# Clustered attention and softplus feed-forward: the value product with its halves side by side

## The chip, the cores and the metric

The kernel runs on one core of a Trainium2 chip. Five engines with queues of their own work side by side: TensorE (PE) multiplies, VectorE (DVE), ScalarE (ACT) and GpSimd (POOL) do the rest, and SyncE (SP) issues the DMAs. The metric is the device time of one execution in microseconds; lower is better. Both kernels compute the same function from the same inputs.

## The reference

Queries and keys are given to the nearest of 16 centroids per head, a query attends only to keys of its own cluster, and the attention's output goes through a feed-forward layer with softplus:

```python
q_assign = np.argmax(np.einsum('bhsd,hcd->bhsc', q_n, c_n), axis=-1)
k_assign = np.argmax(np.einsum('bhsd,hcd->bhsc', k_n, c_n), axis=-1)
mask = q_assign[:, :, :, None] == k_assign[:, :, None, :]
scores = scale * np.matmul(q, k.transpose(0, 1, 3, 2))
scores = np.where(mask, scores, -1000000000.0)
scores = scores - np.max(scores, axis=-1, keepdims=True)
attn = np.exp(scores)
attn = attn / (np.sum(attn, axis=-1, keepdims=True) + 1e-09)
out = np.matmul(attn, v)
...
h = x @ w_in
g = np.maximum(h, 0.0) + np.log1p(np.exp(-np.abs(h)))
return g @ w_out
```

There are 4 batches of 8 heads, 768 tokens, 64 values a head; the layer goes from 512 to 2048 and back to 512. The weights arrive in 64 bits.

## The kernel before

**Halves.** To keep fp32 accuracy at the speed of fp16, a number is held as two fp16 numbers, a high and a low half. A product of two such numbers is three products: high by high, high by low, low by high, summed in PSUM.

**Tiles.** A tile is 128 queries of one head against all 768 keys; there are 192, taken in eight passes of 24 (half a batch's queries, all heads; three tiles a head). `scores` multiplies them on TensorE (line 1021, four products of 384 columns into two PSUM banks), VectorE takes the negative maximum (`negm`, line 1037), ScalarE the exponential (line 1048). The result p is split into halves `phl` by a cast (line 539, any of three engines) and a subtraction (line 529, VectorE or GpSimd), and for two tiles at a time a transposing DMA turns it into `pt`. The first 24 tiles stay in fp32 and are turned on TensorE (line 1065); their exponential also adds up the row's sum.

**Values.** `attend` multiplies pt by the values. For each of the six key blocks of a later tile there are three products (lines 1157 to 1159), all into the same 64 columns: p's high half by v's high half with a column of ones beside it (65 columns; the ones give the row's sum), p's high half by v's low half (64), p's low half by v's high half and ones (65). Six tiles, the three tiles of two heads, stand side by side in one PSUM bank, `mbank`; when the sixth is done VectorE forms 1 / (sum + 1e-9) (lines 1183 and 1185) and scales all six out of PSUM into `x32` (line 1192). The bank is taken for the next six after that.

**Similarities.** `nearest` compares a query or key block with the centroids. From batch 1 on, ten of the twelve blocks of a group take their high and low part in one product of 32 columns (line 761), which VectorE then adds (line 771); for the last two there is no room in the bank, and they take two products each (lines 763, 764).

**Feed-forward.** `ffn1` (lines 1236 to 1238) and `ffn2` (lines 1319 to 1321) run behind attention by about a pass, with softplus on ScalarE, VectorE and GpSimd; `store` adds up two halves (line 1339) and issues the output.

**Order.** Every operation is a step of a generator. A table of numbers, `SEQUENCE`, says which generator issues its next operation (and, by thousands, on which of its possible engines), so the order on every engine's queue is fixed in the program. `Order` follows the issue with a clock of its own; from that it puts warming products into TensorE's expected gaps (line 494, "fills"). Engines run their queues in order and wait on semaphores that the framework sets from the tiles that are read and written.

The start of the kernel prepares keys, queries and weights (rebuilding the 64-bit weights from integer pieces) while the first tiles run.

## Time and profile before

| | |
|---|---|
| Time, median of 3 runs | 825.71 us (824.12 to 825.8) |
| Profiled execution: span, first to last instruction | 824.5 us |
| TensorE busy | 809.5 us, 98% |
| VectorE busy | 647.6 us, 79% |
| ScalarE busy | 567.8 us, 69% |
| GpSimd busy | 444.5 us, 54% |

For the profiled execution the page gives the span alone; the whole time of the timed runs lies about 1.2 us above it. A busy TensorE is one with a product in flight; products overlap, so the step from one start to the next says what a product costs, not its duration. A share of the span is a mean over stages that differ; the rows below are read by stretch.

### The profile page before, as it was taken

What the parts mean: (1) busy time and instruction counts of PE and PEld (TensorE: products, weight loads), DVE (VectorE), ACT (ScalarE), POOL (GpSimd) and SP (SyncE); (2) the same over time, 40 slices, a digit from 0 to 9 for tenths busy, and PEclk for the clock granted to TensorE, in tenths of its full rate; (3) what the DMA queues carried; (4) which work ended last, traced back from release to release, by engine and by line L of the source; (5) the groups of instructions that cost most, each with busy time, mean ns of one, the idle gap of its engine ahead of it and who ended that gap; (6) DMA issues with size and microseconds to landing.
All of it is one profiled execution on the core that took longest, in us unless ns stands there. A gap on an engine that the chain in (4) does not pass through costs nothing.

```text
span 824.5 us, 19467 instructions
## 1 busy us (share of the span) xinstructions
PE 809.5 (98%) x7893; PEld 518.3 (63%) x7893; DVE 647.6 (79%) x1127; ACT 567.8 (69%) x987; POOL 444.5 (54%) x358
## 2 busy tenths in 40 slices
PE   8999988999999999999999999999999999999998
PEld 7888865655656565656565656656666565555553
DVE  8999999998898977898778888887587887743222
ACT  7999998998857667667565746785686664433530
POOL 4325444655367376777685465856777653522320
PEclk9999999999999999999999999999999999999999
DMA  9436999999979999999978989999969874640001
GB/s 327 161 85 168 214 201 228 205 225 177 207 153 187 180 195 205 195 211 193 180 141 155 173 174 183 211 212 175 201 135 169 163 135 103 123 84 14 26 2 38
DMA packets 386314, 134.27 MB, mean 163 GB/s; under 512 B 362672, under 2 KB 379056, under 8 KB 386224
## 3 DMA queue, kind: packets, MB, share of 16 engines
q1 hardware_dynamic: 386224, 133.03, 80.1%
q8 instruction: 61, 1.00, 0.5%
q14 instruction: 29, 0.24, 0.1%
HBM read 35.68 MB, written 6.29 MB: 51 GB/s over the span
## 4 chain that ended last, share of the span: by engine, by line
PE 79%; DMA 4%; DVE 3%; ACT 3%; POOL 1%; issue 1%; DVEq 0%; ACTq 0%; POOLq 0%
PE s L1021 11%; PE h L1236 9%; PE h L1237 9%; PE h L1238 9%; PE o L1321 9%; PE o L1319 9%; PE o L1320 9%; DMA pt<-phl 4%; PE mbank L1157 3%; PE mbank L1159 3%; PE mbank L1158 3%; DVE negm L1037 1%; ACT p L1048 1%; DVE phl L529 1%; ACT phl L539 1%
## 5 line engine op out<-in xcount | busy, mean ns | idle before, releaser
L1048 ACT ACTIVATE p<-s,negm 128x768 f32<-128x768 f32 x190 | 171.9, 908 | 77.9 <-DVE negm L1037 65.6
L1037 DVE TENSOR_REDUCE negm<-s 128x1 f32<-128x768 f32 x192 | 181.7, 951 | 35.4 <-PE s L1021 34.2
L529 POOL TENSOR_TENSOR phl<-p,phl 128x768 f16<-128x768 f32 x81 | 138.2, 1710 | 71.7 <-DVE phl L539 36.0
L1238 PE MATMUL h<-xT,wi 128*128 128x384 f16 x512 | 166.8, 326 | 0.0
L1237 PE MATMUL h<-xT,wi 128*128 128x384 f16 x512 | 166.8, 326 | 0.0
L1236 PE MATMUL h<-xT,wi 128*128 128x384 f16 x512 | 166.7, 326 | 0.0
L1021 PE MATMUL s<-kt,qt 128*128 128x384 f16 x768 | 156.1, 326 | 2.5 <-DVE phl L1111 1.4
L1321 PE MATMUL o<-wo,gh 128*128 128x512 f16 x384 | 146.0, 380 | 0.0
L1320 PE MATMUL o<-wo,gh 128*128 128x512 f16 x384 | 146.0, 380 | 0.0
L1319 PE MATMUL o<-wo,gh 128*128 128x512 f16 x384 | 146.0, 380 | 0.0
L1285 POOL TENSOR_TENSOR fg<-fg,fa 128x384 f32<-128x384 f32 x64 | 69.8, 1094 | 82.9 <-ACT fa L1281 74.9
L1157 PE MATMUL mbank<-vb,pt 128*128 128x65 f16 x1008 | 109.0, 193 | 3.0 <-DMA pt<-phl 3.0
L1158 PE MATMUL mbank<-vb,pt 128*128 128x64 f16 x1008 | 109.1, 192 | 0.0
L1159 PE MATMUL mbank<-vb,pt 128*128 128x65 f16 x1008 | 108.8, 194 | 0.0
L1157 PEld LDWEIGHTS <-pt 128*128 128x128 f16 x1008 | 93.7, 98 | 16.8 <-DMA pt<-phl 5.1
L1021 PEld LDWEIGHTS <-qt 128*128 128x128 f16 x768 | 71.9, 98 | 48.9 <-issue 3.5
L1158 PEld LDWEIGHTS <-pt 128*128 128x128 f16 x1008 | 93.1, 97 | 11.4
L1267 ACT ACTIVATE fa<-h 128x384 f32<-128x384 f32 x82 | 40.2, 491 | 80.7 <-PE h L1238 63.8
L529 DVE TENSOR_TENSOR phl<-p,phl 128x768 f16<-128x768 f32 x81 | 90.6, 1125 | 4.3 <-ACT phl L539 2.2
L1159 PEld LDWEIGHTS <-pt 128*128 128x128 f16 x1008 | 93.2, 97 | 0.0
L539 ACT CAST phl<-p 128x768 f16<-128x768 f32 x92 | 75.2, 828 | 8.3 <-DMA pt<-phl 7.7
L1280 ACT ACTIVATE fa<-fa 128x384 f32<-128x384 f32 x128 | 65.8, 522 | 11.2 <-DVE fa L1263 11.1
(176 smaller groups left out, 1474.0 us busy)
## 6 DMA issues: line engine op xcount, KB each, us to landing
wo<-in_moe_w_in_dram SPq DMA_DIRECT2D x16, 512.0 KB, 6.8
wo<-in_moe_w_out_dram SPq DMA_DIRECT2D x14, 512.0 KB, 4.5
rawk<-in_k_dram SPq DMA_DIRECT2D x16, 384.0 KB, 4.2
rawq<-in_q_dram SPq DMA_DIRECT2D x16, 384.0 KB, 4.4
rawv<-in_v_dram SPq DMA_DIRECT2D x16, 384.0 KB, 4.6
out_dram<-ot SPq DMA_DIRECT2D x24, 256.0 KB, 2.6
pt<-phl SPq DMA_TRANSPOSE x82, 5.9
wraw<-in_moe_w_out_dram SPq DMA_DIRECT2D x2, 512.0 KB, 4.6
```

Of the source, the lines that this page charges most:

```text
L529: [lambda e=e: e.tensor_tensor(dst, a, b, ALU.subtract) for e in (nc.gpsimd, nc.vector)],
L1021: nc.tensor.matmul(st[:, j, :SH], qt[:, s, i], kt[:, s, NT // 2 * j : NT // 2 * (j + 1)], start=(s == 0), stop=(s == 1),)
L1037: yield op("DVE", 950, lambda: nc.vector.tensor_reduce(negm, st[:, :, :SH], AX.XY, ALU.max, negate=True))
L1157: nc.tensor.matmul(av, pt[:, 0, c], vb[:, c, D : 2 * D + 1], start=(c == 0), stop=False)
L1158: nc.tensor.matmul(av[:, :D], pt[:, 0, c], vb[:, c, :D], start=False, stop=False)
L1159: nc.tensor.matmul(av, pt[:, 1, c], vb[:, c, D : 2 * D + 1], start=False, stop=(c == NT - 1))
L1236: nc.tensor.matmul(hp, w[0], x[0], start=(c == 0), stop=False)
L1237: nc.tensor.matmul(hp, w[0], x[1], start=False, stop=False)
L1238: nc.tensor.matmul(hp, w[1], x[0], start=False, stop=(c == NP - 1))
L1319: nc.tensor.matmul(po, g[0], wo[:, f, 0, 0], start=(f == f0), stop=False)
L1320: nc.tensor.matmul(po, g[0], wo[:, f, 0, 1], start=False, stop=False)
L1321: nc.tensor.matmul(po, g[1], wo[:, f, 0, 0], start=False, stop=(f == f0 + NF // 2 - 1))
```

## The change

The value product of the later 168 tiles takes two products a key block instead of three: p's high half by v's low and high halves side by side (128 columns), and p's low half by v's high half (64 columns, added onto the second half of the 128). The two 64-column parts that result are added by VectorE, for two tiles at a time, on the way out of PSUM (`TENSOR_REDUCE`, line 1255 of the new kernel). The bank is cut into two slots of two tiles that take turns. The column of ones goes; ScalarE adds up the row sums of every tile with the exponential. The scaling of a later group then works from SBUF to SBUF, on VectorE or GpSimd. In the later similarities all twelve blocks are joint: the joint results begin at column 8 of the bank, and VectorE adds them in two instructions, the first eight and then the last four, since the later sums overwrite what the first instruction has read. More operations may run on GpSimd (weight preparation, query scaling, masks). The last output tile is multiplied and stored in two parts, 384 and 128 columns. `SEQUENCE` is a new table throughout; the other rank tables are the same.

```diff
--- before.py
+++ after.py
+PAIR = 425
...
 SEQUENCE = [
-    0, 0, 0, 0, 0, 0, 0, 0, 0, 0, 1, 2, 4, 0, 1, 0, 6, 468, 469, 1001, 0, 468, 0, 0, 3, 1, 468, 2004, 1, 0, 468, 1,
...
+    665, 466, 466, 466, 466, 466, 665, 666, 666, 466, 466, 466, 667, 667,
 ]
...
-        vb = cpool.tile([P, 2, NT, 2 * D + 2], F16, name=f"vb{i}")
-        nc.vector.memset(vb[:, :, :, 2 * D :], 1.0)
-        VB.append(vb)
+        VB.append(cpool.tile([P, 2, NT, 2 * D], F16, name=f"vb{i}"))
...
+    def either(dve, pool, f, shared=True):
+
+        if not shared:
+            return op("DVE", dve, lambda: f(nc.vector))
+        return op(
+            ("DVE", "POOL"), (dve, pool), (lambda: f(nc.vector), lambda: f(nc.gpsimd)), shared=True, bias=BIAS
         )
...
-        if joint:
+        for lo, hi in ((0, 8), (8, joint)) if joint else ():
             yield op(
                 "DVE",
-                145 + 35 * joint,
-                lambda: nc.vector.tensor_reduce(sim[:, :joint], wide.rearrange("p c s l -> p c l s"), AX.X, ALU.add),
+                145 + 35 * (hi - lo),
+                lambda: nc.vector.tensor_reduce(
+                    sim[:, lo:hi], wide[:, lo:hi].rearrange("p c s l -> p c l s"), AX.X, ALU.add
+                ),
             )
...
             hk, ps = yield from bank("x", False, [P, 32, NCL], F32, f"sim_q{sfx}")
-            wide = ps[:, nx:].rearrange("p (c s) l -> p c s l", s=2)
+            wide = ps[:, 8:].rearrange("p (c s) l -> p c s l", s=2)
...
             od.drop(hk)
         yield op(
-            "POOL",
-            180 + 1290 * part,
-            lambda: nc.gpsimd.tensor_tensor(n2[:, :, :D], n1[:, :, :D], aq.to_broadcast([P, nx, D]), ALU.mult),
+            ("POOL", "DVE"),
+            (180 + 1290 * part, 130 + DQA * part),
+            [
+                lambda e=e: e.tensor_tensor(n2[:, :, :D], n1[:, :, :D], aq.to_broadcast([P, nx, D]), ALU.mult)
+                for e in (nc.gpsimd, nc.vector)
+            ],
             shared=True,
...
-        tot = {}
-        if whole(t):
-            if n // 2 not in sums:
-                sums[n // 2] = p2.tile([P, 2 * nt, 1], F32, tag="sum", name=f"sum_{n}", bufs=NP)
-            tot["accum_out"] = sums[n // 2][:, n % 2 * nt + i]
-        yield op("ACT", 1000 if whole(t) else 898, lambda: nc.scalar.activation(ex, st[:, :, :SH], AF.Exp, bias=negm, **tot))
+        if (n // 2, pi) not in sums:
+            sums[n // 2, pi] = p2.tile([P, 2 * nt, 1], F32, tag="sum", name=f"sum_{n}_{pi}", bufs=NP)
+        total = sums[n // 2, pi][:, n % 2 * nt + i]
+        yield op("ACT", 1000, lambda: nc.scalar.activation(ex, st[:, :, :SH], AF.Exp, bias=negm, accum_out=total))
...
-        if h % 2 == 0 and i == 0:
-            avs["k"] = yield from ring("m", 1)
-            avs["t"] = mbank[:, : 2 * nt * (D + 1)].rearrange("p (h c d) -> p h c d", h=2, c=nt)
-        av = avs["t"][:, h % 2, i]
+        od.mread = math.inf
+        t0 = t - t % (2 * nt)
+        if whole(t):
+            if t == t0:
+                avs[t] = [(yield from ring("m", 2))]
+                avs[t].append((yield from ring("m", 2)))
+            av = mbank[:, (t - t0) * D : (t - t0 + 1) * D]
+        else:
+            if t % 2 == 0:
+                avs[t] = [(yield from ring("m", 2))]
+            slots = mbank.rearrange("p (u c s d) -> p u c s d", u=2, c=2, s=2)[:, t // 2 % 2]
+            av = slots[:, t % 2].rearrange("p s d -> p (s d)")
 
         def emit():
             if whole(t):
                 vf = raw_v[n - n % 2][0][:, n % 2]
                 for c in range(NT):
-                    nc.tensor.matmul(av[:, :D], pt[:, c], vf[:, c], start=(c == 0), stop=(c == NT - 1))
+                    nc.tensor.matmul(av, pt[:, c], vf[:, c], start=(c == 0), stop=(c == NT - 1))
                 return
             for c in range(NT):
 
-                nc.tensor.matmul(av, pt[:, 0, c], vb[:, c, D : 2 * D + 1], start=(c == 0), stop=False)
-                nc.tensor.matmul(av[:, :D], pt[:, 0, c], vb[:, c, :D], start=False, stop=False)
-                nc.tensor.matmul(av, pt[:, 1, c], vb[:, c, D : 2 * D + 1], start=False, stop=(c == NT - 1))
-
-        yield op("PE", 1290 if whole(t) else 548, emit)
+                nc.tensor.matmul(av, pt[:, 0, c], vb[:, c, : 2 * D], start=(c == 0), stop=False)
+                nc.tensor.matmul(av[:, D:], pt[:, 1, c], vb[:, c, D : 2 * D], start=False, stop=(c == NT - 1))
+
+        yield op("PE", 1290 if whole(t) else 514, emit)
         od.set(("at", t))
-        if t % 2:
-            od.set(ptk)
-        if h % 2 == 0 or i < nt - 1:
+        if t % 2 == 0:
+            return
+        od.set(ptk)
+        if not whole(t):
+            if t - t0 == 1:
+                xk = yield from ring("x32", 1)
+                avs["x", t0] = xk, p2.tile([P, 2 * nt, D], F32, name=f"x32_{n}_{pi}", **own(xk, 1))
+                od.set(("x32", t0))
+            else:
+                yield wait("x32", t0)
+                yield wait("xp", t - 2)
+            xk, xf = avs["x", t0]
+            part = xf[:, t - 1 - t0 : t + 1 - t0]
+            yield op("DVE", PAIR, lambda: nc.vector.tensor_reduce(part, slots.rearrange("p c s d -> p c d s"), AX.X, ALU.add))
+            od.set(avs[t - 1][0])
+            od.set(("xp", t))
+        if t + 1 - t0 < 2 * nt:
             return
         if pi == 0:
             yield wait("v", n - 1)
             od.set(raw_v[n - 1][1])
         if last[pi]:
             od.set(vkey[n // 2])
-        od.mread = math.inf
-
-        mk, avt = avs["k"], avs["t"].rearrange("p h c d -> p (h c) d")
         rs = p2.tile([P, 2 * nt, 1], F32, tag="rs", name=f"rs_{n}_{pi}")
-        t0 = t - t % (2 * nt)
-        kinds = [whole(t0 + c) for c in range(2 * nt)]
-        c = 0
-        while c < 2 * nt:
-            e = next((e for e in range(c, 2 * nt) if kinds[e] != kinds[c]), 2 * nt)
-            weights = sums[n // 2][:, c:e] if kinds[c] else avt[:, c:e, D:]
-            dst = rs[:, c:e]
-            yield op("DVE", 155, lambda: nc.vector.tensor_scalar(dst, weights, 1e-9, None, ALU.add), shared=kinds[c])
-            c = e
+        yield op("DVE", 155, lambda: nc.vector.tensor_scalar(rs, sums[n // 2, pi], 1e-9, None, ALU.add), shared=True)
         yield op("DVE", 190, lambda: nc.vector.reciprocal(rs, rs))
-        xk = yield from ring("x32", 1)
-        x32 = p2.tile([P, 2, nt, D], F32, name=f"x32_{n}_{pi}", **own(xk, 1))
-        xf = x32.rearrange("p h c d -> p (h c) d")
-        yield op(
-            "DVE",
-            550,
-            lambda: nc.vector.tensor_tensor(xf, avt[:, :, :D], rs.to_broadcast([P, 2 * nt, D]), ALU.mult),
-        )
-        od.set(mk)
-        od.mread = od.cur["now"]
+        wide = rs.to_broadcast([P, 2 * nt, D])
+        if whole(t):
+            xk = yield from ring("x32", 1)
+            xf = p2.tile([P, 2 * nt, D], F32, name=f"x32_{n}_{pi}", **own(xk, 1))
+            src = mbank[:, : 2 * nt * D].rearrange("p (c d) -> p c d", d=D)
+            yield op("DVE", 550, lambda: nc.vector.tensor_tensor(xf, src, wide, ALU.mult))
+            for key in avs[t0]:
+                od.set(key)
+        else:
+            yield op(
+                ("DVE", "POOL"),
+                (550, 920),
+                [lambda e=e: e.tensor_tensor(xf, xf, wide, ALU.mult) for e in (nc.vector, nc.gpsimd)],
+                shared=True,
+                bias=BIAS,
+            )
+        x32 = xf.rearrange("p (h c) d -> p h c d", h=2)
...
+        CUT = DM * 3 // 4
+        ends = pi == len(passes) - 1 and half and i == nt - 1
+        sides = [slice(0, CUT), slice(CUT, DM)] if ends else [slice(0, DM)]
...
+            if ends and side is sides[0]:
+                od.spawn(store(pi, half, i, po, ok, side), od.cur["prio"])
+        od.spawn(store(pi, half, i, po, ok, sides[-1]), od.cur["prio"])
...
```

On TensorE, where the 30th pair of later tiles (the last two tiles of batch 1's fourth head) multiplies its second tile. `s` is a score product, `pt` the turned p, `mbank` the value bank; a row in brackets waits for a semaphore of the engine named. Before:

```order
L1021 LDWEIGHTS qt_3_4464
L1021 MATMUL s_5_5296<-kt_2917,qt_3_4464 128x384
L1157 LDWEIGHTS pt_5_5143
L1157 MATMUL mbank<-vb_103,pt_5_5143 128x65
L1158 LDWEIGHTS pt_5_5143
L1158 MATMUL mbank<-vb_103,pt_5_5143 128x64
L1159 LDWEIGHTS pt_5_5143
L1159 MATMUL mbank<-vb_103,pt_5_5143 128x65
L1157 LDWEIGHTS pt_5_5143
```

There the tile's first product waits for nothing. The same place in the changed kernel, from the last product of the pair's first tile on:

```order
L1238 LDWEIGHTS pt_5_4823
L1238 MATMUL mbank<-vb_102,pt_5_4823 128x64
L1095 LDWEIGHTS qt_3_4246
L1095 MATMUL s_5_4987<-kt_2715,qt_3_4246 128x384 [waits Activation_49]
L1095 LDWEIGHTS qt_3_4246
L1095 MATMUL s_5_4987<-kt_2715,qt_3_4246 128x384
L1095 LDWEIGHTS qt_3_4246
L1095 MATMUL s_5_4987<-kt_2715,qt_3_4246 128x384
L1095 LDWEIGHTS qt_3_4246
L1095 MATMUL s_5_4987<-kt_2715,qt_3_4246 128x384
L1237 LDWEIGHTS pt_5_4823
L1237 MATMUL mbank<-vb_102,pt_5_4823 128x128 [waits DVE_49]
```

Two products a key block stand in place of three, and the second tile's first product waits for VectorE with four score products ahead of it.

On VectorE, the end of that group of six tiles (`x`, `rs`: the group's output and reciprocal sums). Before, all that the group asks of VectorE:

```order
L1183 TENSOR_SCALAR rs_3_5351<-mbank 128x6 [waits PE_49]
L529 TENSOR_TENSOR phl_5_5257<-p_13_3_5278,phl_5_5257 128x768 [waits DMAHW3_49,Activation_49]
L539 CAST phl_4_5390<-p_13_5_5385 128x768 [waits DMAHW7_49,Activation_49]
L1185 RECIPROCAL rs_3_5351<-rs_3_5351 128x6 [waits DVE_49]
L1192 TENSOR_TENSOR x_11_3_5416<-mbank,rs_3_5351 128x384 [waits DVE_49]
```

In the changed kernel, around the second pair sum of the group, the one that the product above waits for:

```order
L1111 TENSOR_REDUCE negm_3_4888<-s_3_4855 128x1
L1439 SCALAR_TENSOR_TENSOR ot_4_4179<-o_4_1_4706,ot_4_4179 128x512 [waits PE_49]
L1363 TENSOR_SCALAR fg_3_4964<-h_6_4903 128x384 [waits Activation_49]
L1255 TENSOR_REDUCE x_10_3_4824<-mbank 128x128 [waits PE_49]
L1111 TENSOR_REDUCE negm_4_4955<-s_4_4887 128x1
L1374 TENSOR_TENSOR fg_2_4801<-fg_2_4801,fa_5_4882 128x384 [waits Activation_49]
L1111 TENSOR_REDUCE negm_5_4996<-s_5_4987 128x1 [waits PE_49]
```

The bank is read three times a group, two tiles at a time, instead of once, and each read stands among the maxima and the softplus of other tiles.

## Rows read from the trace of the kernel before

**Rows 1.** The page, section 1: busy time, share of the span and instructions.
```profile
PE 809.5 (98%) x7893; PEld 518.3 (63%) x7893; DVE 647.6 (79%) x1127; ACT 567.8 (69%) x987; POOL 444.5 (54%) x358
```
**Rows 2.** Busy time by stretch: length, then each engine's us, granted clock, DMA share, GB/s.
```profile
60.00:100.00 40.00, 38.83 (x364) 33.98 (x364) 39.39 (x70) 39.94 (x81) 17.95 (x17) 1.00 0.80 189
100.00:140.00 40.00, 35.18 (x378) 23.83 (x376) 38.05 (x64) 36.32 (x62) 19.09 (x15) 0.96 1.04 221
140.00:200.00 60.00, 60.00 (x613) 37.51 (x610) 57.55 (x102) 55.42 (x94) 32.79 (x26) 1.00 0.96 198
200.00:300.00 100.00, 99.61 (x1018) 61.87 (x1017) 87.57 (x137) 71.86 (x119) 55.19 (x41) 1.00 0.99 183
715.00:825.00 110.00, 105.81 (x648) 55.85 (x646) 38.26 (x62) 39.41 (x82) 25.08 (x23) 1.00 0.16 37
```
**Rows 3.** TensorE's waits, 0 to 140 us, then 140 to 825: total, times, longest.
```profile
PE mbank L1157 <- DMA pt<-phl: 2.3, 1, 2.3
...
PE mbank L1157 <- DMA pt<-phl: 0.8, 2, 0.4
```
**Rows 4.** Busy time by stretch, around the fall of the granted clock (0.57).
```profile
129.00:133.00 4.00, 4.00 (x27) 2.29 (x24) 3.87 (x5) 3.76 (x7) 1.27 (x1) 0.57 0.81 182
```
**Rows 5.** TensorE in order of time, a value tile: start us, us, instruction.
```profile
405.90 0.19 PE L1157 MATMUL mbank<-vb,pt 128*128 128x65 f16 x1
405.93 0.20 PE L1158 MATMUL mbank<-vb,pt 128*128 128x64 f16 x1
405.96 0.19 PE L1159 MATMUL mbank<-vb,pt 128*128 128x65 f16 x1
...
406.44 0.81 PE L1021 MATMUL s<-kt,qt 128*128 128x384 f16 x4
```
**Rows 6.** TensorE in order of time: six transposes and what follows.
```profile
10.15 0.50 PE L744 MATMUL kT<-eye,kn 128*128 128x128 f16 x6
10.48 0.58 PE L494 MATMUL mbank<-ones,eye 128*128 128x120 f16 x8
```
**Rows 7.** TensorE in order of time: the similarities of one key block.
```profile
212.09 0.41 PE L761 MATMUL sim_k<-cents,kt 128*128 128x32 f16 x10
212.34 0.17 PE L763 MATMUL sim_k<-cents,kt 128*128 128x16 f16 x1
212.37 0.17 PE L764 MATMUL sim_k<-cents,kt 128*128 128x16 f16 x1
```
**Rows 8.** All engines in order of time, the end of the span.
```profile
820.43 0.38 PE L1321 MATMUL o<-wo,gh 128*128 128x512 f16 x1
820.85 0.69 DVE L1339 SCALAR_TENSOR_TENSOR ot<-o,ot 128x512 f32<-128x512 f32 x1 [4.49 <-PE o L1321]
821.57 0.33 SPq L1342 DMA_DIRECT2D out_dram<-ot  x1
```
**Rows 9.** VectorE by line: shapes, count, busy us, mean ns, idle before.
```profile
L1037 DVE TENSOR_REDUCE negm<-s 128x1 f32<-128x768 f32 x192 | 181.7, 951 | 35.4 <-PE s L1021 34.2
L529 DVE TENSOR_TENSOR phl<-p,phl 128x768 f16<-128x768 f32 x81 | 90.6, 1125 | 4.3 <-ACT phl L539 2.2 <-POOL phl L539 1.9
L1192 DVE TENSOR_TENSOR x<-mbank,rs 128x384 f32<-128x384 f32 x32 | 17.7, 552 | 0.8
L771 DVE TENSOR_REDUCE sim_q<-sim_q 128x160 f32<-128x320 f32 x12 | 5.9, 495 | 1.8 <-PE sim_q L764 1.8
```
**Rows 10.** The page, section 6: the output's stores, KB each, us to landing.
```profile
out_dram<-ot SPq DMA_DIRECT2D x24, 256.0 KB, 2.6
```
**Rows 11.** TensorE by line: the fills in the value bank.
```profile
L494 PE MATMUL mbank<-ones,eye 128*128 128x120 f16 x148 | 10.7, 216 | 0.0
```
**Rows 12.** GpSimd by line: the softplus sum.
```profile
L1285 POOL TENSOR_TENSOR fg<-fg,fa 128x384 f32<-128x384 f32 x64 | 69.8, 1094 | 82.9 <-ACT fa L1281 74.9
```
**Rows 13.** ScalarE in order of time: an exponential that reads out its sum.
```profile
23.87 0.90 ACT L1048 ACTIVATE p<-s,negm 128x768 f32<-128x768 f32 x1
24.67 0.19 ACT L1048 ACTIVATION_READ_ACCUMULATOR p<-s,negm 128x1 f32 x1
24.77 0.75 ACT L670 ACTIVATE wo<-wo,down 128x512 int32<-128x512 uint16 x1
```

More of the change, by code (lines that the diff above doesn't have):

```diff
@@ L29 @@
 WIDE = 1
+PSC = 1560
+PQS = 1950
+DQA = 830
+DCP = 365
+PCP = 820
 EBIAS = 200
@@ L369, in pump, with lock, start @@
         self.cur = outer
-    def start(self, ch, eng):
+    def lock(self, eng, asked, ns):
+        other = self.shared["POOL" if eng == "DVE" else "DVE"]
+        start, later = asked, []
+        for i, x in enumerate(other):
+            if x[2] <= asked:
+                continue
+            if x[0] > asked:
+                later = other[i:]
+                break
+            start = max(start, x[2])
+        if later:
+            delay = start + ns - later[0][1]
+            if delay > 0:
+                self.free["POOL" if eng == "DVE" else "DVE"] += delay
+                for x in later:
+                    x[1] += delay
+                    x[2] += delay
+        self.shared[eng] = self.shared[eng][-63:] + [[asked, start, start + ns]]
+        return start
+    def start(self, ch, eng, ns):
         t = max(ch["now"], self.free[eng])
         if ch["op"][4].get("shared") and eng in self.shared:
-            t = max(t, self.shared["POOL" if eng == "DVE" else "DVE"])
+            t = self.lock(eng, t, ns)
         return t
@@ L383, in run @@
                 eng, ns, emit = eng[which], ns[which], emit[which]
-            start = self.start(ch, eng)
+            start = self.start(ch, eng, ns)
             if eng == "PE" and self.warm:
@@ L387, in run @@
             self.free[eng] = start + ns - self.PIPE[eng]
-            if opt.get("shared") and eng in self.shared:
-                self.shared[eng] = start + ns
             end = start + ns + self.LAT[eng]
@@ L779, in nearest @@
         half = 140 + 10 * nt
-        yield op("DVE", half if hit else ns, lambda: nc.vector.tensor_tensor(w, w, tab[:, :nt], ALU.mult), shared=bool(hit))
+        slow = 180 + 27 * nt
+        yield either(half if hit else ns, slow, lambda e: e.tensor_tensor(w, w, tab[:, :nt], ALU.mult), bool(hit))
         best = p2.tile([P, nt, 1], F16, tag="best", name=f"best_{sfx}", bufs=4)
@@ L917, in prep_q @@
         n1 = p2.tile([P, nx, P], F16, name=f"qn1_{sfx}", **own(k1, 2))
-        yield op("ACT", 120 + 720 * part, lambda: nc.scalar.activation(n1[:, :, :D], qf, AF.Copy, scale=SCALE))
+        yield op(
+            ("ACT", "DVE", "POOL"),
+            (120 + 720 * part, 145 + 420 * part, 178 + PQS * part),
+            (
+                lambda: nc.scalar.activation(n1[:, :, :D], qf, AF.Copy, scale=SCALE),
+                lambda: nc.vector.tensor_scalar(n1[:, :, :D], qf, SCALE, None, ALU.mult),
+                lambda: nc.gpsimd.tensor_scalar(n1[:, :, :D], qf, SCALE, None, ALU.mult),
+            ),
+            shared=True,
+        )
         yield op(
@@ L1337, in store @@
             return
+        share = (side.stop - side.start) / DM
+        at, from_ = acc[:, side], po[:, side]
         yield op(
-            "DVE", 680, lambda: nc.vector.scalar_tensor_tensor(acc, po, 1.0 / SW2, acc, ALU.mult, ALU.add)
-        )
-        od.drop(ok)
-        yield op("SP", 500, lambda: nc.sync.dma_start(out_v[b, :, c0 + i], acc), load=256e3 / 290)
-        od.set(ak)
+            "DVE",
+            130 + 550 * share,
+            lambda: nc.vector.scalar_tensor_tensor(at, from_, 1.0 / SW2, at, ALU.mult, ALU.add),
+        )
+        if side.stop == DM:
+            od.drop(ok)
+        yield op("SP", 500, lambda: nc.sync.dma_start(out_v[b, :, c0 + i, side], at), load=share * 256e3 / 290)
+        if side.stop == DM:
+            od.set(ak)
     def chain_of(gens):
```

102 lines of the change are left out of this document (62 added, 40 removed), and 330 rows, old and new, of the table SEQUENCE.

## The prediction

> **What bounds the kernel now.** I read the page's busy shares first, then the busy time by stretch, then what TensorE waits for, then single instructions. TensorE is busy 98% of the 824.5 us [rows 1]. By stretch it falls into two halves. From 60 to 140 us VectorE is busy 39.39 of 40 and 38.05 of 40 us and ScalarE 39.94 and 36.32, and TensorE has holes (35.18 of 40 us from 100 to 140). From 140 us on TensorE has none: 60.00 of 60, then 99.61 of 100, with VectorE at 57.55 of 60 and then 87.57 of 100 [rows 2]. The waits say the same: up to 140 us the longest TensorE wait is 2.3 us for a transposing DMA, and from 140 us to the end all its waits on others add up to 0.8 us [rows 3]. So after 140 us a microsecond of TensorE work taken away is a microsecond won, as long as nothing makes TensorE wait; before 140 us VectorE and ScalarE have to get shorter. One row more: from 129 to 133 us TensorE is granted 0.57 of its clock, the 1.2 GHz level for most of it, right after the stretch with holes [rows 4]; elsewhere it is at 2.4 GHz. I count that episode, some 1.7 us, as staying.
>
> **The change part by part**, against the profiled execution (span 824.5 us; the median of the three timed runs, 825.71, lies 1.2 above it, and I apply the differences to the median).
>
> *Value products.* A tile of 18 products takes from 405.90 to 406.44, 0.54 us, so 30 ns a product [rows 5]. The new tile has six products of 128 columns and six of 64. The nearest row for 128 columns with a weight load each is the on-chip transposes: six from 10.15 to 10.48, 55 ns each [rows 6]; 64 columns cost 30 ns as now. 6 x (55 + 30) = 510 ns, 30 ns less, on 192 - 24 = 168 tiles: 5.0 us. Bounds: the narrow product can stand at 28 to 33 ns (single steps of the old tile) and the wide one at 55 to 56, so 498 to 534 ns, 7.0 to 1.0 us. All of it is TensorE time, nearly all behind 140 us, so I count it in full.
>
> The Trainium skill's page "TensorE: Matmul & The Clock Gate" (section Back-to-back issue gap) speaks against this part: in a stream of weight loads and products it puts a 128-column product at about 81 ns, and by that the tile would grow to some 670 ns and the kernel by some 20 us. The transposes in this trace are such a stream and take 55 ns, so the trace does not agree and I give it nothing.
>
> *Similarities.* From 212.09 ten joint products take 0.25 us, and the four narrow ones for the last two blocks take another 25 ns each [rows 7]. Two blocks in each of 24 groups now need one product instead of two: 48 x 25 ns = 1.2 us of TensorE. Their sum on VectorE becomes two instructions (counted below).
>
> *The end.* The last matmul of 512 columns starts at 820.43 and lasts 0.38, the sum after it 0.69, then comes the store [rows 8]. With only 128 columns left the matmul drains 384 x 0.42 = 160 ns sooner, and the sum, at about 1.02 ns an element and 0.17 fixed (from 951 ns for 768 and 495 for 320 [rows 9]), takes 0.30. That is 0.55 less; 24 more products at 2.5 ns overhead give back 0.06. The store is a quarter as large; its 2.6 us to landing [rows 10] I leave as it is (between 0 and 1 us less). Together -0.5 us.
>
> *Fills.* The order has 190 warming products against 216: 26 x 53 ns = 1.4 us of TensorE (148 of one kind took 10.7 us of overlapping busy time [rows 11]; 53 ns is their step). A fill that goes may leave only a wait, so I take half, -0.7; bounds 0 and -1.4.
>
> *VectorE and ScalarE.* 84 pair sums are added; by the same line 256 elements cost 0.43 us (bounds: 0.32, a third of the 768-element row, and 0.50, the 320-element row), 36 us. The split similarity sum adds 24 x 0.22 = 5 us. Sixteen scalings stay on VectorE reading SBUF, at the old 0.55, and 12 go to GpSimd (about 1.09 us there by the softplus sum of the same size) [rows 9, 12]; eleven of the 1.1 us subtractions go as well, some casts come in. Net about +40 us of VectorE, so its 87.57 of 100 becomes some 92 of 100. 166 exponentials now read out their sum: the row shows the read-out starting at 24.67 and the next instruction at 24.77, so 0.1 us each, up to 0.19 if nothing overlaps [rows 13]: 17 to 32 us of ScalarE, on which 71.86 of 100 were busy. From 200 us this lies beside TensorE. From 140 to 200 us, where VectorE has 2.45 us left [rows 2], about nine more pair sums (3.9 us) fall due; some of that must show. I take +1.0 us for the whole kernel. Ends: -1 (less for VectorE to do between 140 and 200 where work moved to GpSimd) to +7 (every one of the 13 or so pair sums up to 200 us on the path, and a microsecond of read-outs).
>
> *One bank, a new wait.* The two slots that the pair sums alternate between lie in one PSUM bank, and the program treats the bank as one object: in the new order 62 of the 84 pairs have a TensorE product that waits for VectorE, and it is the sum of the pair just before, not the one two back. Before, one product in each group of six tiles had such a wait, and no row of VectorE stands among TensorE's waits after 140 us [rows 3]. Behind the waiting product stands everything on TensorE's queue. What hides the wait is the TensorE work between the pair's last product and the waiting one: by the order it is 1.6 us or more almost everywhere, but 0.5 to 1.3 us in some 14 places (in the TensorE rows shown above four score products, 0.65 us). The chain is 0.19 (drain, rows 5) + 0.04 (matmul end to VectorE start, 820.81 to 820.85 [rows 8]) + 0.43 + about 0.04 back = 0.70 us with VectorE free, and about 0.4 more for the instruction it is in. So the 14 places lose 0 to 0.6 us each. I take 0.14 on average, +2.0 us; bounds 0 and 14 x 0.6 = 8.
>
> The page "PSUM — Partial Sum Buffer" of the Trainium skill (section on bank collisions) gives the reason for such a wait: PSUM is to be guarded by bank and quadrant, not by address, since two engines in one bank collide. The order agrees; what a collision does, no run here shows.
>
> *Sum.* -5.0 - 1.2 - 0.5 - 0.7 + 1.0 + 2.0 = -4.4; 825.7 - 4.4 = 821.3 us.
>
> **Rivals.** (a) *The bank's waits eat the gain.* For: 62 waits where 28 groups had one, each behind a VectorE that will be over 90% busy. Against: most have over 1.6 us of cover. Price 14 x 0.5 = 7 instead of 2.0: 826.3, and 824 to 826 with part of it; no difference to speak of.
> (b) *VectorE becomes the bound between 60 and 240 us: slower.* There it is busy 95 to 98% [rows 2], and in program order its work ahead of the 57th score maximum grows by about 3.5 us at the durations of the trace, with TensorE's work ahead of that place only 0.9 us shorter. It decides once more than about 7 us of VectorE work lands on the path: 13 pair sums (5.6 us) + four split sums (0.9) + read-outs and waits (4) = 10.5 in place of 3.0: 825.7 + 3.1 = 828.8. Against: by the 65th maximum the two orders ask the same of VectorE (262.6 and 262.8 us by those sums).
> (c) *The start gets shorter too.* Weight and query preparation can now go to GpSimd, which is busy 19.09 of 40 us from 100 to 140 [rows 2], and the first stage has 134 fills in place of 177. Against: VectorE's work ahead of the 39th maximum is 155.0 us by the trace's durations, against 153.6. If 5 us of the holes go: 816.3.
>
> **How the numbers follow.** The forecast 0.56, (a) 0.16, (b) 0.11, (c) 0.17. A change under 0.2% (1.65 us) is about what a measurement of this kernel cannot tell from none. Faster: 0.53 of the forecast, 0.04 of (a), all of (c): 0.74. Within 0.2%: 0.03 + 0.11 + 0.01 = 0.15. Slower: 0.01 of (a) and 0.10 of (b): 0.11. The range, 815 to 827, takes in (c), most of (a), and the ends of the value products; (b) lies outside.
>
> **What would show it.** Right: a value tile of about 0.51 us from first start to next; TensorE's waits after 140 us at 2 to 4 us, with VectorE's pair sum (from PSUM to x) named as the releaser in a few places under 0.7 us each; VectorE at 90 to 94% from 200 to 715 us; the last matmul to the end about 0.5 us shorter. Wrong: tiles of 0.53 us or more; TensorE under 58 of 60 us busy from 140 to 200 (rival b); or pair-sum waits adding up to 6 us (rival a); or TensorE's holes before 140 us shrunk by over 3 us (rival c).

## The result, and the profile after

The changed kernel takes 831.09 us (median of four runs, 830.74 to 831.36); the kernel before, on the same chip, 825.75 (824.12 to 826.16). The ratio is 1.0075, with a 95% interval of 1.0061 to 1.0089: slower by 5 to 7 us, 5.3 by the medians. The forecast was 821.3 us with a range up to 827; it was wrong in sign, and the time lies outside the range.

The page of the changed kernel, section 1, in the columns of [rows 1]:

```profile
PE 803.6 (97%) x6835; PEld 511.0 (62%) x6835; DVE 667.7 (80%) x1228; ACT 595.5 (72%) x1167; POOL 421.8 (51%) x350
```

TensorE has 1058 matmuls fewer and is busy 5.9 us less, in a span that is 4.9 us longer. So it is not work that costs, but standing. Where it stands, the busy time by stretch says; first the kernel before in the stretches that [rows 2] do not hold:

```profile
300.00:400.00 100.00, 99.94 (x1016) 61.62 (x1012) 83.33 (x138) 69.24 (x118) 74.61 (x58) 1.00 1.06 197
400.00:500.00 100.00, 100.00 (x998) 61.45 (x997) 80.13 (x122) 62.70 (x105) 62.91 (x50) 1.00 0.88 166
500.00:600.00 100.00, 100.00 (x991) 61.20 (x989) 76.00 (x137) 66.33 (x108) 65.13 (x51) 1.00 1.04 196
600.00:700.00 100.00, 99.59 (x1000) 61.41 (x998) 79.25 (x122) 64.75 (x109) 59.32 (x46) 1.00 0.76 144
```

and the changed kernel, same view:

```profile
100.00:140.00 40.00, 34.10 (x346) 23.57 (x346) 38.25 (x70) 37.91 (x74) 22.60 (x18) 1.00 1.02 226
140.00:200.00 60.00, 58.61 (x504) 36.24 (x502) 57.97 (x108) 56.21 (x108) 32.27 (x27) 1.00 0.97 199
200.00:300.00 100.00, 98.22 (x839) 60.43 (x838) 85.57 (x149) 77.18 (x153) 51.08 (x39) 1.00 0.93 179
300.00:400.00 100.00, 97.40 (x810) 58.43 (x808) 87.17 (x158) 72.31 (x140) 62.08 (x48) 1.00 1.02 194
400.00:500.00 100.00, 97.27 (x829) 59.87 (x827) 89.13 (x148) 71.98 (x140) 43.22 (x32) 1.00 0.89 172
500.00:600.00 100.00, 99.43 (x829) 59.86 (x827) 81.38 (x153) 66.35 (x130) 69.33 (x54) 1.00 0.98 187
600.00:700.00 100.00, 98.38 (x820) 60.40 (x818) 76.97 (x130) 71.36 (x142) 60.61 (x47) 1.00 0.78 144
```

From 300 to 700 us TensorE's holes add up to 400 - 399.53 = 0.5 us before and 400 - 392.48 = 7.5 us after; from 140 to 300 they go from 0.4 to 3.2. The path of before, TensorE without a gap from 140 us on, is broken into. From 200 us on VectorE is nowhere over 90%, so it is not the bound by its mean, and its fullest stretches there (300 to 500 us) are those with the largest holes. The clock is granted in full throughout; the episode of [rows 4] has gone.

What TensorE waits for, over the whole span of the changed kernel (total us, times, longest):

```profile
PE mbank L1237 <- DVE x L1255: 7.1, 8, 1.8
PE s L1095 <- ACT p L1120: 4.4, 8, 1.8
PE mbank L1237 <- DMA pt<-phl: 2.6, 3, 1.0
...
PE o L1413 <- DVE ot L1439: 0.6, 1, 0.6
```

The first row is new: eight value products stood 7.1 us for the pair sum (line 1255) that VectorE makes in the same bank. From 140 us on all of TensorE's waits add up to 10.9 us, 5.5 of them for the sum, against 0.8 before [rows 3]. I had looked for a few waits for the sum, each under 0.7 us; the longest is 1.8. That one can be read in order of time, on TensorE first. The rows begin with the second tile of a pair:

```profile
348.30 0.22 PE L1237 MATMUL mbank<-vb,pt 128*128 128x128 f16 x1
348.36 0.19 PE L1238 MATMUL mbank<-vb,pt 128*128 128x64 f16 x1
...
348.78 0.19 PE L1238 MATMUL mbank<-vb,pt 128*128 128x64 f16 x1
348.81 0.38 PE L1413 MATMUL o<-wo,gh 128*128 128x512 f16 x1
...
355.08 0.38 PE L1415 MATMUL o<-wo,gh 128*128 128x512 f16 x1
357.22 0.22 PE L1237 MATMUL mbank<-vb,pt 128*128 128x128 f16 x1 [1.76 <-DVE x L1255]
```

and VectorE in the same stretch:

```profile
348.92 0.37 DVE L836 TENSOR_TENSOR sim_q<-sim_q,tab 128x192 f32<-128x192 f32 x1
...
351.30 0.96 DVE L1049 TENSOR_TENSOR n<-qn,aq 128x768 f16<-128x768 f16 x1
352.17 0.55 DVE L1374 TENSOR_TENSOR fg<-fg,fa 128x384 f32<-128x384 f32 x1
352.64 0.55 DVE L1363 TENSOR_SCALAR fg<-h 128x384 f32<-128x384 f32 x1
353.11 0.95 DVE L556 TENSOR_TENSOR kn<-rawk,kn 128x768 f16<-128x768 f32 x1
353.98 0.95 DVE L556 TENSOR_TENSOR gh<-fg,gh 128x768 f16<-128x768 f32 x1
354.85 1.99 DVE L1374 TENSOR_TENSOR fg<-fg,fa 128x384 f32<-128x384 f32 x1
356.76 0.41 DVE L1255 TENSOR_REDUCE x<-mbank 128x128 f32<-128x256 f32 x1
```

The tile itself takes 0.51 us (348.30 to 348.81), as forecast. Its pair's last product drained at 348.97. The sum began at 356.76, 7.8 us later, since a dozen other steps stood ahead of it in VectorE's order and filled it without a gap. TensorE had over 6 us of other work as cover, used it up at about 355.3, and stood until the sum was done at 357.17. For all 84 pairs, the time from the end of the pair's last product to the start of its sum is 1.1 us in the median, 4.6 at the ninth tenth, and 7.8 at most.

The sums themselves, in the view of one line (durations in ns; idle time in us, times):

```profile
L1255 DVE TENSOR_REDUCE x<-mbank x84: 408/415/427, 109.8 to 740.7; 128x128 f32<-128x256 f32 x84
...
its engine sat idle before it (us, times) until:
  PE mbank L1238: 10.8, 16
  POOL xn L556: 0.8, 3
who waited for it (us, times):
  PE mbank L1237: 7.1, 8
```

A sum costs 0.415 us, against the 0.43 taken. It couples the two engines in both directions: VectorE stands for the products (10.8 us), and TensorE for the sum. The first of the two is hardly new: before, VectorE stood 9.1 us for the products at the one read of each group (line 1183). TensorE's wait is the new one.

### The profile page after: what moved, and what is told of

It is laid out like the page before. It is cut to its first block, busy times and chain, and to the rows that moved or that the text cites. A ratio compares the mean times of both kernels' runs of the same rounds, so it can differ in the third digit from the quotient of the medians.

```text
span 829.4 us, 17632 instructions
## 1 busy us (share of the span) xinstructions
PE 803.6 (97%) x6835; PEld 511.0 (62%) x6835; DVE 667.7 (80%) x1228; ACT 595.5 (72%) x1167; POOL 421.8 (51%) x350
## 4 chain that ended last, share of the span: by engine, by line
PE 66%; DVE 9%; DMA 5%; ACT 3%; issue 3%; POOL 0%; SPq 0%; DVEq 0%; ACTq 0%; POOLq 0%
PE s L1095 9%; PE h L1325 8%; PE h L1327 8%; PE h L1326 8%; PE o L1413 8%; PE o L1415 8%; PE o L1414 8%; PE mbank L1237 5%; DMA pt<-phl 4%; PE mbank L1238 3%; DVE negm L1111 2%; ACT p L1120 1%; DVE phl L556 1%; DVE fg L1374 1%; DVE x L1255 1%
## 5 line engine op out<-in xcount | busy, mean ns | idle before, releaser
L556 POOL TENSOR_TENSOR phl<-p,phl 128x768 f16<-128x768 f32 x92 | 155.0, 1691 | 108.7 <-ACT phl L574 77.7
L1413 PE MATMUL o<-wo,gh 128*128 128x512 f16 (+2 forms) x392 | 146.6, 375 | 0.6 <-DVE ot L1439 0.6
L1414 PE MATMUL o<-wo,gh 128*128 128x512 f16 (+2 forms) x392 | 146.5, 375 | 0.0
L1415 PE MATMUL o<-wo,gh 128*128 128x512 f16 (+2 forms) x392 | 146.5, 375 | 0.0
L1237 PE MATMUL mbank<-vb,pt 128*128 128x128 f16 x1008 | 107.7, 220 | 9.9 <-DVE x L1255 7.1
L1238 PE MATMUL mbank<-vb,pt 128*128 128x64 f16 x1008 | 103.3, 193 | 0.0
L574 ACT CAST phl<-p 128x768 f16<-128x768 f32 x113 | 92.6, 829 | 13.6 <-DMA pt<-phl 11.8
L1238 PEld LDWEIGHTS <-pt 128*128 128x128 f16 x1008 | 87.6, 98 | 20.7 <-issue 9.6
L1237 PEld LDWEIGHTS <-pt 128*128 128x128 f16 x1008 | 89.7, 98 | 16.2 <-DMA pt<-phl 4.1
L1356 ACT ACTIVATE fa<-h 128x384 f32<-128x384 f32 x86 | 42.0, 488 | 64.2 <-PE h L1327 48.2
L556 DVE TENSOR_TENSOR phl<-p,phl 128x768 f16<-128x768 f32 x70 | 70.2, 1012 | 1.5 <-ACT phl L574 1.2
L1326 PEld LDWEIGHTS <-wi 128*128 128x128 f16 x512 | 50.1, 98 | 33.7 <-issue 1.3
L1327 PEld LDWEIGHTS <-wi 128*128 128x128 f16 x512 | 50.1, 98 | 33.4 <-issue 0.3
```

Of the source, the lines that this page charges most:

```text
L556: [lambda e=e: e.tensor_tensor(dst, a, b, ALU.subtract) for e in (nc.gpsimd, nc.vector)],
L1237: nc.tensor.matmul(av, pt[:, 0, c], vb[:, c, : 2 * D], start=(c == 0), stop=False)
L1238: nc.tensor.matmul(av[:, D:], pt[:, 1, c], vb[:, c, D : 2 * D], start=False, stop=(c == NT - 1))
L1326: nc.tensor.matmul(hp, w[0], x[1], start=False, stop=False)
L1327: nc.tensor.matmul(hp, w[1], x[0], start=False, stop=(c == NP - 1))
L1413: nc.tensor.matmul(out_, g[0], wo[:, f, 0, 0, side], start=(f == f0), stop=False)
```

## Experiments

The theories. **One bank:** TensorE stands at the next pair's product until VectorE, which comes late to the sum of the pair just before, has read the bank. **VectorE's load:** the sums make VectorE late everywhere, wherever the wait then shows. **Read-outs:** the row sums read out on ScalarE are the price. Ratios are to the kernel before, on the same chip. Where a constant stands for data, the kernel leaves the right result out, and its time alone is of use.

**Sums that do not read the bank.** Same size and place in VectorE's order, but from a constant in SBUF (`still` is `eye32`, viewed in the shape of the two slots):

```diff
-nc.vector.tensor_reduce(part, slots.rearrange("p c s d -> p c d s"), AX.X, ALU.add)
+nc.vector.tensor_reduce(part, still, AX.X, ALU.add)
```

> The changed kernel, with the 84 pair sums of the same shape reading a constant tile in SBUF instead of the value bank (the value product's result is left out); VectorE keeps the same instructions in the same order. 'One bank' (the value product waits for a late pair sum, because both slots lie in one bank): the 7.1 us of waits on the sum go, 831.1 falls to 823 to 825. 'VectorE's load' (the added sums make it late for everything): no change, 830 to 832. 'Read-outs' (ScalarE's added sums): no change, 830 to 832.

Measured: 824.29 us, ratio 0.9975 (0.9959 to 0.9991). The sums still took 0.41 us each on VectorE; only the bond with the bank was gone, in both directions, and with it some 8 us (1.0075 against 0.9975).

**No read-outs** in the 168 exponentials of later tiles; a constant stands for the row sums:

```diff
+        if not whole(t):
+            sums[n // 2, pi] = unit
...
-AF.Exp, bias=negm, accum_out=total))
+AF.Exp, bias=negm, **(dict(accum_out=total) if whole(t) else {})))
```

> The changed kernel without the sum's read-out in the exponentials of the 168 later tiles (a constant stands for the row sums). 'Read-outs': the 4.4 us of score products waiting for an exponential shrink to some 1 us, 826 to 828. 'One bank': 0 to 1.5 us less, 829.5 to 831. 'VectorE's load': the same, 829.5 to 831.

Measured: 833.13 us, 1.0084 (1.006 to 1.0108). Nothing comes back.

**The kernel before with a read-out in every exponential**, unused in the later tiles:

```diff
+        else:
+            tot["accum_out"] = p2.tile([P, 1], F32, tag="extra", name=f"extra_{sfx}", bufs=4)
```

> The kernel before, with a row sum read out in every exponential (unused in the 168 later tiles). 'Read-outs': 825.75 rises by 3 to 5 us, 829 to 831. 'One bank' and 'VectorE's load': 0 to 1.5 us more, 826 to 827.

Measured: 826.59 us, 0.9999 (0.9987 to 1.0011). The two together put the read-outs out of the question, to within about 1 us.

**The kernel before with 84 sums from SBUF on VectorE**, unused, one behind the VectorE step that follows each pair:

```diff
+    od.extra = lambda: nc.vector.tensor_reduce(spare, still, AX.X, ALU.max)
...
+            if eng == "DVE" and self.owed:
+                self.owed -= 1
+                self.extra()
```

> The kernel before, with 84 sums of 256 elements added to VectorE (from SBUF into a spare tile, one behind the next VectorE instruction after each pair's second value product), about 35 us of VectorE work that nothing waits for. 'VectorE's load': 825.75 rises by 4 to 8 us, 830 to 834. 'One bank' and 'Read-outs': 0 to 2 us more, 826 to 828.

Measured: 829.47 us, 1.0031 (1.0017 to 1.0045). So VectorE's load by itself costs, about 2.6 us, between the 4 to 8 of its own theory and the 0 to 2 of the others. Where it shows: TensorE's waits from 140 us on, in this kernel,

```profile
PE mbank L1165 <- DMA pt<-phl: 2.6, 3, 1.4
PE mbank L1165 <- DVE x L1201: 0.6, 1, 0.6
```

that is, mostly in transposing DMAs that come later; before, they had 0.8 us [rows 3]. The likely reason is that VectorE, which writes part of their source, wrote it later; this was not followed step by step.

**The same with sums that read the value bank:**

```diff
+            two = mbank[:, c1 - D - 1 : c1 + D + 1].rearrange("p (c d) -> p c d", c=2)[:, :, :D]
...
+            od.owed.append(lambda: nc.vector.tensor_reduce(spare.rearrange("p (c d) -> p c d", c=2), two, AX.X, ALU.max))
```

> The kernel before with 84 further VectorE sums of 256 elements, as in the run with sums from SBUF (ratio 1.0031), but these read the two slots of each tile pair in the PSUM bank of the value results, so value products of the next pairs wait for them; what they write is not used. 'One bank': the waits of value products on VectorE appear and it costs several us on top of the 2.6: 830 to 836 us, ratio 1.006 to 1.012. 'VectorE's load': the same as with sums from SBUF, 828 to 830 us, ratio 1.002 to 1.0045.

Measured: 857.01 us, 1.0365 (1.0346 to 1.0384), far over the 836 expected. The bank costs in this kernel too, but by the other direction of the bond. VectorE's waits (total, times, longest):

```profile
DVE spare L1174 <- PE mbank L1164: 44.5, 42, 2.9
```

Here the sum stands close behind its products in VectorE's order, so VectorE stands 44.5 us for TensorE, and what TensorE needs from VectorE comes late; direct waits of products on the spare sums are 1.2 us only. It shows that a sum in the bank can be dear when it comes early as well, and it is no measure of the changed kernel's own loss.

**Value products held back.** In writing TensorE's order, a value product that would wait for the pair's sum goes behind later steps, until 3 or 6 us of TensorE work stand in between:

```diff
+            if held is None and code % 1000 in self.value and self.summed and self.cover < 3000:   # or 6000
+                if self.active[code % 1000]["op"][1] == "PE":
+                    held = code
+                    continue
```

> The changed kernel with the same work, but in TensorE's order a value product that would wait for the sum of the pair before is held back behind later TensorE steps, until 3.0 us of TensorE work (by the order's own numbers) stand between the two. Theory 'One bank' (VectorE comes late to the pair sum and TensorE stands at the next value product): waits of value products on the pair sum fall from 7.1 to 2-4 us; 824 to 828 us, ratio 0.993 to 0.997 to the changed kernel, 1.000 to 1.003 to the kernel before. 'VectorE's load' (VectorE is too busy, wherever the wait shows): the waits only move to score and other products, 829 to 832 us, ratio 1.005 or more to the kernel before.

> The same with 6.0 us of TensorE work between the two. 'One bank': the waits of value products on the pair sum nearly vanish (under 2 us in all, since the largest lag of a sum seen was 7.8 us and nine in ten are under 4.6); 822 to 826 us, ratio to the kernel before 0.996 to 1.000. 'VectorE's load': 829 to 832 us again, or more, since the value results come later too.

Measured: 832.01 us, 1.008 (1.0064 to 1.0096), and 835.0 us, 1.0103 (1.0087 to 1.0119). By "One bank" these two should have brought 3 to 9 us; they brought none. TensorE's waits with 6 us:

```profile
PE s L1117 <- ACT p L1142: 8.2, 12, 2.1
PE mbank L1259 <- DMA pt<-phl: 3.0, 3, 1.2
PE h L1349 <- ACT fg L1388: 2.2, 4, 1.1
...
PE mbank L1259 <- DVE x L1279: 1.3, 2, 0.9
```

The waits on the sum did fall, from 7.1 to 1.3 us, and came back as waits for exponentials (4.4 to 8.2) and for the feed-forward's ScalarE. As I read it, the step that goes ahead in place of a held product has its own wait, and what follows from the product comes later. More cover in the order was no cure, and by the numbers expected these two runs speak for "VectorE's load"; the first experiment and the next one speak against it.

**Waits two pairs back.** Sums from SBUF again, so that the value result is left out, but VectorE still waits for the products, and TensorE still waits for a sum, that of two pairs back, through a small tile of its own for each of the two slots:

```diff
+            if t % 2:
+                nc.tensor.matmul(av[:, :16], eye, gates[t // 2 % 2][:, :16], start=True, stop=True)
...
+nc.vector.tensor_reduce(gates[t // 2 % 2].rearrange("p (c d) -> p c d", c=2), still, AX.X, ALU.max)
```

> The changed kernel with pair sums that read a constant in SBUF (as in the run with sums from SBUF, 0.9975), but in which VectorE still waits for the pair's products: a product of 16 columns behind each pair reads a small tile of its slot, which the sum writes. TensorE then waits for the sum two pairs back and no longer for that of the pair just before. The value result is left out of the output. Theory 'TensorE waits' (what costs is TensorE standing at the next value product until a late sum is done): the 84 small products add 84 x 25 ns = 2.1 us to 824.3, so 825 to 828 us, ratio 0.999 to 1.002. Rival 'VectorE waits' (what costs is VectorE, in order, standing at the sum until the products are done: 10.8 us in the changed kernel, and all that is late behind it): 829 to 834 us, ratio 1.004 or more, with TensorE's waits on scores and transposes grown.

Measured: 824.32 us, 0.998 (0.9969 to 0.9992), just under what "TensorE waits" asked for, with 84 products more than the changed kernel. VectorE still stands 5.6 us at the sums for the products; no product stands for a sum:

```profile
L1264 DVE TENSOR_REDUCE gate<-eye x84: 399/409/421, 109.8 to 732.0; 128x128 f16<-128x256 f32 x84
its engine sat idle before it (us, times) until:
  PE mbank L1247: 5.6, 8
who waited for it (us, times):
```

and TensorE is closed again, by stretch:

```profile
300.00:400.00 100.00, 99.22 (x846) 60.20 (x844) 87.39 (x163) 74.50 (x143) 63.32 (x50) 1.00 1.04 198
400.00:500.00 100.00, 100.00 (x848) 61.35 (x847) 87.12 (x150) 73.38 (x145) 45.99 (x37) 1.00 0.89 174
500.00:600.00 100.00, 100.00 (x857) 60.76 (x856) 82.23 (x159) 69.13 (x135) 67.06 (x52) 1.00 0.99 187
600.00:700.00 100.00, 100.00 (x851) 61.88 (x850) 77.28 (x129) 69.63 (x140) 58.00 (x47) 1.00 0.81 150
```

Holes from 300 to 700 us: 0.8, against 7.5 in the changed kernel, with nearly the same VectorE load (334.0 us in that stretch against 334.7). So what costs is TensorE's wait for the sum of the pair just before. VectorE's wait for the products is halved here, but with it gone altogether, in the first experiment, the time is no shorter. (The scalings read a constant here and no longer wait for the sum; in the first experiment they did, and the time is the same. The wait two pairs back was never felt: no product stood for it.)

**Value products in 18 again**, in the changed kernel's order, without pair sums; one or two scalings a group read the bank. And the same for the first 96 tiles alone:

```diff
+            if narrow(t0):
+                for c in range(NT):
+                    nc.tensor.matmul(av, pt[:, 0, c], vb[:, c, :D], start=(c == 0), stop=False)
+                    nc.tensor.matmul(av, pt[:, 0, c], vb[:, c, D : 2 * D], start=False, stop=False)
+                    nc.tensor.matmul(av, pt[:, 1, c], vb[:, c, D : 2 * D], start=False, stop=(c == NT - 1))
+                return
```

> The changed kernel with the value products in 18 products of 64 columns again, added on TensorE, no pair sums, one VectorE scaling a group out of the bank (two where a group wraps round the eight slots); read-outs, similarities, end and the order of the rest as in the changed kernel. TensorE has 168 x 42 ns = 7 us more to do at the step of 30 ns (85.5 against 92.5 us in the traces). If the pair sums (bank wait and VectorE's load, 8 + 2.6 us by the two runs before) are the whole loss: 831 + 7 - 10.6 = 827.5, so 825 to 829 us, ratio 0.999 to 1.004. If other parts of the change (order, similarities, end, read-outs) lose too: 832 us or more, ratio 1.007 or more.

> Half of each: the groups of the first 96 tiles with 18 products and no pair sums, the later ones with 12 and pair sums, as changed. VectorE is busiest up to 300 us, which the first half covers, but the holes of the changed kernel lie between 200 and 500 us on both sides of the cut (tile 96 starts at 358.7 us). 'The pair sums are the loss' with a price that is even over the tiles: between the two, 827 to 830 us, ratio 1.001 to 1.005. If the price is paid mainly where VectorE is full (before 300 us): under 826 us, ratio 0.996 to 1.000, and this one would be the best kernel.

Measured: 840.89 us, 1.0183 (1.0169 to 1.0198), and 831.32 us, 1.0065 (1.0051 to 1.0079). The first lies where I had expected it if other parts of the change lose too (832 or more), and 9 us above that bound; the second misses both of its expectations and is no faster than the changed kernel, though its products stand for sums and scalings for only 3.1 us. I do not take the first as a clean undoing. TensorE's waits in it:

```profile
PE mbank L1253 <- DVE x L1304: 4.2, 3, 2.9
PE mbank L1253 <- DVE x L1306: 3.5, 3, 1.4
```

Six products stand 7.7 us for the scalings, the one reader of the bank that is left. As I read it, this order is written for two slots and puts the next group's products ahead of where the scaling comes. But 831.1 + 7 for the added products - 10.6 for the pair sums + 7.7 for these waits is about 835, and not 840.9: some 6 us are not explained, and these two runs do not show that the pair sums are the whole loss. What the rest of the change does is read better from the two runs with sums from SBUF.

**The last tile in one part:**

```diff
+                    if ends and side is sides[0]:
+                        return
+                    side = slice(0, DM)
...
```

> The changed kernel with the last output tile finished in one part again. The trace of the changed kernel shows an end shorter by 1.1 us behind the last matmul and a new hole of 0.6 to 0.8 us ahead of it. If these two are all that the split does: 0 to 0.8 us slower than the changed kernel, 830.5 to 832 us, ratio to the kernel before 1.006 to 1.009. If the split is behind the loss, it would be 2 us or more faster than the changed kernel, under 829 us.

Measured: 832.02 us, 1.0072 (1.006 to 1.0084), the same as the changed kernel: the split end is worth nothing, to within about 1 us.

**Sums moved ahead in VectorE's order**, once 1.2 or 2.4 us of TensorE work stand behind the pair:

```diff
+                    if self.active[seq]["op"][4].get("pair") and seq != code % 1000:
+                        if self.busy - self.done[seq] >= 1200:   # or 2400
+                            ahead.add(seq)
+                            self.issue(seq)
```

> The changed kernel with one rule more in writing VectorE's order: a pair sum goes ahead of the step that would be next on VectorE as soon as 1.2 us of TensorE work (the order's own numbers) stand behind the pair's last product. The work is the same, the result whole. 'The order' (the sum is late because other steps stand ahead of it): TensorE's waits on sums fall from 7.1 to under 2.5 us, 824 to 828 us, ratio 0.998 to 1.003. 'VectorE is full' (what is moved back behind the sum is late instead): waits move to scores, transposes and feed-forward products, 829 to 833 us, ratio 1.004 to 1.009.

> The same rule from 2.4 us of TensorE work on, so that fewer sums are moved and VectorE stands less often at a sum whose products are not done. 'The order': TensorE's waits on sums 2 to 4 us, 825 to 829 us, ratio 0.999 to 1.004, near the version from 1.2 us. 'VectorE is full': as the changed kernel or a little better, 829 to 832 us.

Measured: 850.0 us, 1.03 (1.0282 to 1.0318), and 845.35 us, 1.0244 (1.0224 to 1.0263). Far worse than either theory. VectorE's waits at the sums in the first:

```profile
...
DVE x L1272 <- PE mbank L1255: 22.3, 19, 4.2
...
DVE x L1272 <- POOL xn L573: 14.4, 8, 5.2
```

A sum that comes early stands for its products (22.3 us, against 10.8) and for GpSimd, which still reads the one x buffer that the sum writes (14.4 against 0.8). TensorE's waits on the sum fell only to 5.9 us. So the late place of the sum is not an oversight of the order that moving it by this rule mends: it stands between two waits. No version that computes the whole result and beats the kernel before came out of this. The runs from SBUF suggest that slots in two banks would be one, but scores and the other products hold the other seven banks; it was not tried.

## Why the prediction was wrong

The step that failed is **"One bank, a new wait"**: the mechanism and its bank were right, the size was not. I took +2.0 us, with 0 to 8 as bounds. The products' direct waits for the sum alone measured 7.1 us. The two runs in which no product stands for a sum differ from the changed kernel by 1.0075 - 0.9975 = 1.0%, 8 us, and by 1.0075 - 0.998 = 0.95%, 8 us, with 84 x 29 ns = 2.4 us of added products still in the latter (29 ns is their median step there). So it is 8 to 10 us, give or take 2, at or over my upper bound. Two assumptions made it small:

- The chain "0.70 us with VectorE free, and about 0.4 more for the instruction it is in". A sum waits for every step that stands ahead of it in VectorE's order, not for one. The gap behind the products, 0.04 + 0.4 in my chain, measured 1.1 us in the median and up to 7.8. The order of the changed kernel could be read beforehand; I counted cover on TensorE in it and not the steps on VectorE in the same stretch.
- The "14 places" with little cover. The place shown above had over 6 us of cover and still lost 1.76 us. With cover of 1.6 us and more "almost everywhere", I had called the other 48 waiting pairs safe. Of the eight waits in the trace, five (3.5 us) have 1.6 us of cover or more; three (3.6 us) have less, and a dozen places with less lost nothing. Where the wait falls is decided by VectorE's queue as much as by the cover.

The other steps:

- *Value products*, -5.0: right, rather more. The time from matmul start to matmul start, summed over their lines, was 92.8 us, 92.4 without the waits in it, and is 90.8, 85.6 without 5.2 us of waits: -7, the far end of my range for it. The 81 ns that the Trainium skill's page "TensorE: Matmul & The Clock Gate" (section Back-to-back issue gap) gives for 128 columns are not borne out here either: the first two rows of the tile stand 0.06 us apart, and a 128-column product takes 57 ns to the next start in the median.
- *VectorE and ScalarE*, +1.0: the read-outs are free to within 1 us. The sums' load alone cost 2.6 us in the kernel before, most of it seen at later transposing DMAs, a path that I had not named. My "+40 us of VectorE" does not follow from its own terms: 36 + 5, less 12 scalings (6.6) and eleven subtractions (12.1), is some 22, and the pages show 667.7 - 647.6 = 20.1; from 200 to 300 us VectorE is busy 85.57 of 100, not 92.
- *The end*, -0.5: 0. From the last matmul's start to the end of the span it did shrink, 824.5 - 820.43 = 4.1 us to 829.4 - 826.41 = 3.0, but the second part's first product stood 0.65 us for the first part's sum in the same bank, again a bank wait, and the run in one part takes as long.
- *Fills*, -0.7: from 100 to 140 us TensorE is busy 34.10 us in place of 35.18 [rows 2], and 1.4 us of fills are gone. A fill that goes leaves a wait; nothing shows that they gave anything.
- *Similarities*, -1.2: no run takes them alone.
- *The clock* of [rows 4], counted as staying at some 1.7 us: the changed kernel's trace has 1.00 from 129 to 133 us. No run takes this alone.

With these sizes: -7 - 1.2 + 0 + 0 + 2.6 + 8 = +2.4, against +5.3 by the medians. By these numbers the remaining 3 us lie outside the bank's wait: without its 8 us the terms come to -5.6, but the run with sums from SBUF, where no product stands for a sum, lies at 0.9975, only 2.1 us below the kernel before. TensorE's waits from 140 us on in that run,

```profile
PE mbank L1239 <- DMA pt<-phl: 3.5, 4, 1.4
PE s L1097 <- ACT p L1122: 1.1, 2, 0.9
PE o L1415 <- DVE ot L1441: 0.6, 1, 0.6
```

are 5.2 us in place of 0.8 [rows 3]: 4.4 more, where I have put 2.6 for VectorE's load. What makes these DMAs and exponentials late in the new order no run shows, and the rest stays open.

The page "PSUM — Partial Sum Buffer" of the Trainium skill (section on bank collisions) asks for guards by bank and quadrant. The trace agrees that this program waits by bank, and the runs give the price of it; what a collision without the guard would do, no run shows.

Among the rivals, (a) named the cause, at 7 us and 826.3, with the advantage of all other terms as forecast, and its sign came: waits on the sum over 6 us. (b), VectorE as the bound, has the right direction but not the cause: with nearly the same VectorE load and the wait gone, the kernel is faster than before, and from 140 to 200 us TensorE is busy 58.61 of 60, above the 58 that was (b)'s sign. (c) did not come: the holes before 140 us did not shrink by 3 us.

## What to carry to other kernels

Double buffering counts in the unit that the program's waits are made in: here two slots in one bank are one buffer, and an order written for two then waits for the slot just used. Price a new wait by what stands ahead of the releasing step in its own engine's queue, read from the order of both engines for the same stretch, and not by the releasing step's duration. An addition moved from a full engine to another in-order engine can buy, with its microseconds, a bond in both directions (here 10.8 and 7.1 us); a run in which the step is the same size but reads something else tells the bond from the load.

## What was not expected of the hardware

A VectorE addition of two float32 tiles of 384 took 0.55 us at 352.17 and 1.99 us at 354.85, with the same shape, line and names. During the long one GpSimd was in a step of its own on SBUF (same view, GpSimd):

```profile
354.17 2.25 POOL L556 TENSOR_TENSOR phl<-p,phl 128x768 f16<-128x768 f32 x1 [3.25 <-ACT phl L574]
```

The VectorE step ended 0.42 us after the GpSimd step did. It is not the only place. Of VectorE's 64 additions of this shape on line 1374, seven took 0.9 us or more; each of the seven began while a GpSimd step ran, and ended 0.41 to 0.42 us after that step. None of the other 57 (0.55 us in the median) began with more than 0.1 us of a GpSimd step to go. In the kernel before it is 14 of 64, with the same 0.41 us. So in these traces such a VectorE step that meets a running GpSimd step is held until that step is over; no run was made to take it away, and what the two share is not shown. The one above fell just ahead of a sum that TensorE stood for, and by an estimate from the two durations that wait would have been about 0.3 us without it rather than 1.76.
